# A hand-written order of 1,127 pieces, laid anew: chunked attention with a gated convolution on one core

## The chip, the core and the metric

The kernel runs on one core of a Trainium2 chip. The time is device microseconds (us) of one execution. Before the change the median of 3 runs is 266.01 us (265.45 to 266.56). The engines are PE (TensorE, matmuls), DVE (VectorE), ACT (ScalarE), POOL (GpSimd) and SP, whose queue issues every DMA of this kernel.

## The reference

There are 8 batches, 8 heads, 576 tokens and 64 columns a head. Attention stays inside chunks of 64 tokens; its output, with the heads side by side (512 columns), goes through a gate made by a 5-tap causal convolution over the tokens, a value projection and an output projection, all in f32:

```
scores = scale * (q_c @ k_c.T);  scores -= max(scores)
attn = exp(scores);  attn /= attn.sum() + 1e-09
x = (attn @ v_c)                      # -> (B, S, 512)
gate = sigmoid(sum_k conv_w[k] * x[t - 4 + k])
out = (gate * (x @ w_val)) @ w_out    # two 512 x 512 weights
```

## The kernel before, in words

The 4,608 tokens are taken in nine groups of 512, `g` = 0 to 8. A group's heads come in two halves, `p` = 0, 1, and its 512 columns in four slices of 128 (`c`, `m` or `hp`, 0 to 3). Nothing loops over them: the string `ORDER` lists 1,127 pieces of work, one after the other, and each engine gets its instructions in the order in which they stand there (`keep_in_program_order`). So the table decides what stands behind what on each engine, and a piece that has to wait holds up all that follows it on its engine. The table `SLOTS` (a string of buffer numbers for each name) says which buffer each tile gets. A load goes to one of six buffers `ld` or, for weights, one of four `acc`, and can be issued only when the buffer's last reader is done; SP issues in the order of the table too.

The pieces named below (numbers behind a name are g, then p or a slice):

- `lq`, `lk`, `lv`: loads of q, k, v, 512 KB each. `lw v c`, `lw o c`: load of a 128-row slice of w_val or w_out, 512 KB. The weights arrive as 64-bit words and are put together on the chip.
- `w1` to `w7`, `wb`: the steps of that for one slice. `w1` (POOL or DVE), `w3` and `w5` (ACT) read the loaded buffer; `w7` adds the parts to the f32 weight; `w6` (ACT) and `wb` make its high and low parts `v_hi`, `v_lo`. A `G` behind a name puts the piece on POOL, a `D` on DVE.
- `S` scores (PE, 32 or 64 small matmuls of 64x64), `mx` maximum and `sb` subtraction (DVE), `ex` exponential (ACT), `sm` sum and reciprocal (DVE), `nm` normalization (POOL, or DVE as `nmD`), `T` transpose (PE), `ec` copy of it (ACT), `A` times v (PE, 64 small matmuls). `ea` is the exponential by rows on ACT (16 instructions). Group 0, half 0 runs `S`, `mx`, `T`, `A` and so on in two parts.
- `sp`, `ep`, `xn`, `xe`: for group 0, half 1, the subtraction of maximum and high part is done by PE and ACT.
- `xc`, `xr`, `xd`: from PSUM the copy of x (ACT), its high part (ACT), its low part (DVE).
- `k0` (ACT, POOL or DVE) and `k` (DVE): the five taps of the convolution; `sg` its tanh (ACT).
- `V g m c`: value projection, three matmuls of 512 columns (high x high, low x high, high x low); `F 0 m c` does the same for group 0 with f32 operands as two matmuls.
- `vc`/`gs` or `gm`, `gr`, `gd`: the gated value and its high and low part. `P g t c`: output projection, three matmuls. `oc` copies it out of PSUM, `st` stores it.
- `W n`: n matmuls on a tile of zeros, `zr`, `zi`, `zw`, `zm`: constants.

Work of several groups is in flight at once: group 0 begins with its loads while the weights are still being put together, and from about group 1 on scores of a later group, value matmuls of one and output matmuls of an earlier one stand mixed on PE.

Of the kernel before, what the change touches and what calls it, by code (L numbers as in the profile page):

```python
# [17 lines left out]
ORDER = """lk 0 0,lq 0 0,lc,lw v 0,zr 0,w1G c 0,zw,lk 0 1,S 0 0 1,mx 0 0 1,S 0 0 0,zi,sb 0 0 1,mx 0 0 0,ex 0 0 1,zr 1,lq 0 1,  # L18
w5 v 0,sb 0 0 0,lw v 2,W 5,sm 0 0 1,w1G v 0,nm 0 0 1,w3 c 0,zm,ex 0 0 0,w5 c 0,S 0 1 0,w2 v 0,sm 0 0 0,lv 0 0,S 0 1 1,
w3 v 0,lw v 1,mx 0 1,w3 v 2,lk 1 0,nm 0 0 0,w1G v 2,w5 v 2,w2 c 0,hl 0,lq 1 0,w4 v 0,w4 c 0,T 0 0 0,w7 v 0,ec 0 0 0,  # L20
T 0 0 1,w1 v 1,mh 0 1,w9,A 0 0 0,w2 v 2,xc 0 0 0,lw o 3,w3 v 1,ml 0 1,w2 v 1,sp 0 1,ep 0 1,F 0 2 0,lw v 3,ec 0 0 1,
w4 v 2,lq 1 1,w4 v 1,k0 0 0,w7G v 2,w6 v 2,F 0 3 0,F 0 1 0,sm 0 1,w5 v 1,w7G v 1,A 0 0 1,lv 0 1,S 1 0 0,w1G v 3,
xc 0 0 1,w3G o 3,k 0 0 1,w6 v 0,nmD 0 1,lk 1 1,S 1 0 1,F 0 0 0,T 0 1,mx 1 0,k0 0 1,w5 o 3,F 0 1 1,lw o 0,w5 v 3,
w3 v 3,w1G o 3,F 0 3 1,sb 1 0,ec 0 1,ex 1 0,wb v 2,A 0 1,w2 v 3,k 0 0 4,k 0 0 2,xc 0 1 1,sm 1 0,w1G o 0,xc 0 1 0,
S 1 1 0,w3 o 0,lk 2 0,lq 2 0,xr 0 1,nm 1 0,S 1 1 1,F 0 2 1,k0 0 2,lw o 2,xn 0 1,xe 0 1,mx 1 1,sb 1 1,F 0 0 1,ex 1 1,
w4 v 3,V 0 2 2,V 0 1 2,w7G v 3,k 0 2 3,w5 o 0,sm 1 1,S 2 0 0,S 2 0 1,w3G o 2,w2 o 3,w6 v 3,T 1 0,w6 v 1,ec 1 0,mx 2 0,
V 0 0 2,lk 2 1,V 0 3 2,lq 2 1,lv 1 0,wb v 3,k 0 2 2,lv 1 1,S 2 1 0,sb 2 0,k 0 0 3,S 2 1 1,w2 o 0,ex 2 0,mx 2 1,nm 1 1,
A 1 0,V 0 0 3,k0 0 3,V 0 3 3,xr 1 0,sm 2 0,wb v 0,xc 1 0 1,sb 2 1,vc 0 3,V 0 1 3,V 0 2 3,xc 1 0 0,T 1 1,w1G o 2,
xd 1 0,ex 2 1,V 1 3 0,ec 1 1,sm 2 1,lk 3 0,lq 3 0,vc 0 1,S 3 0 0,S 3 0 1,nm 2 0,k 0 1 2,lw o 1,w2 o 2,wb v 1,A 1 1,
sg 0 0,nm 2 1,xc 1 1 0,V 1 3 1,mx 3 0,lv 2 0,gm 0 0,V 1 1 0,xc 1 1 1,hl 1,lk 3 1,ng 3 0,k 0 2 1,w1G o 1,lk 4 0,  # L30
V 1 1 1,V 1 2 0,xr 1 1,V 1 2 1,xd 1 1,V 1 3 2,w4 o 2,V 1 2 2,V 1 1 2,V 1 3 3,k 0 3 2,V 1 1 3,k 0 2 4,w4 o 0,k 0 1 3,
ea 3 0,k 0 3 4,k 0 1 1,w2 o 1,vc 1 3,T 2 1,lq 3 1,w3G o 1,T 2 0,vc 1 1,rc 3 0,k 0 3 3,w4 o 1,ec 2 0,V 1 0 0,V 1 0 1,
ec 2 1,w5 o 1,S 3 1 0,S 3 1 1,k 0 3 1,A 2 0,V 1 0 2,V 1 2 3,sg 0 2,w5 o 2,k 0 1 4,lq 4 0,mx 3 1,xr 2 0,vc 1 2,w7G o 1,
lv 2 1,sb 3 1,lq 4 1,ex 3 1,V 1 0 3,sg 0 3,k0 1 1,A 2 1,xd 2 0,w4 o 3,V 2 2 0,V 2 3 0,vc 1 0,xc 2 0 0,xc 2 0 1,lq 5 0,
w7 o 0,V 2 3 1,V 2 0 0,gm 0 2,V 2 2 1,V 2 0 1,xr 2 1,lv 3 1,lk 4 1,S 4 0 0,k0 1 2,nm 3 0,sm 3 1,S 4 0 1,gs 0 3,w6 o 1,
xd 2 1,gr 0 2,V 2 2 2,mx 4 0,k0G 1 0,sg 0 1,w7G o 2,k 1 1 3,V 2 0 2,V 2 0 3,w6 o 2,gr 0 0,gs 0 1,gdD 0 0,xc 2 1 0,
xc 2 1 1,sb 4 0,V 2 3 2,w6 o 0,V 2 1 0,w7G o 3,V 2 1 1,w6 o 3,k 1 0 1,S 4 1 0,nm 3 1,S 4 1 1,mx 4 1,k 1 0 4,gr 0 1,
gd 0 2,T 3 1,k 1 1 1,V 2 1 2,k 1 2 2,lv 3 0,vc 2 0,ec 3 1,wb o 0,ng 4 1,wb o 1,k 1 1 4,gdD 0 1,V 2 2 3,lk 5 1,k0 1 3,
k 1 2 3,V 2 1 3,P 0 2 0,vc 2 2,wbD o 2,P 0 1 0,hl 2,k 1 2 1,vc 2 1,k 1 0 3,V 2 3 3,k 1 3 4,k 1 1 2,k 1 3 1,P 0 0 0,
ea 4 1,P 0 0 1,rc 4 1,P 0 2 1,lq 5 1,vc 2 3,P 0 2 2,lk 5 0,P 0 0 2,wbD o 3,k 1 3 3,ex 4 0,T 3 0,k 1 2 4,P 0 1 1,  # L40
ec 3 0,P 0 3 0,A 3 1,k 1 3 2,A 3 0,P 0 3 1,xr 3 1,gr 0 3,k 1 0 2,xr 3 0,xc 3 0 0,sm 4 0,P 0 3 2,xc 3 0 1,P 0 1 2,
gd 0 3,sg 1 3,xcD 3 1 0,P 0 1 3,P 0 0 3,P 0 2 3,xc 3 1 1,sg 1 0,P 0 3 3,xd 3 0,oc 0 1,S 5 0 0,S 5 0 1,oc 0 0,oc 0 2,
xd 3 1,oc 0 3,S 5 1 0,S 5 1 1,V 3 3 0,gs 1 0,V 3 0 0,V 3 2 0,nm 4 1,gr 1 0,k0G 2 2,V 3 0 1,V 3 0 2,V 3 3 1,V 3 2 1,
V 3 0 3,sg 1 2,mx 5 0,V 3 3 2,mx 5 1,V 3 1 0,V 3 1 1,sb 5 0,k0 2 3,nm 4 0,T 4 0,ng 5 1,V 3 2 2,k0 2 1,V 3 2 3,V 3 3 3,
sg 1 1,ea 5 1,T 4 1,vc 3 0,vc 3 3,ec 4 0,gs 1 1,gr 1 1,gd 1 0,P 1 3 0,hl 3,lk 6 0,P 1 2 0,V 3 1 2,k 2 3 2,k 2 2 1,
V 3 1 3,k 2 1 3,lq 6 0,gs 1 2,gr 1 2,k0 3 1,lv 5 0,S 6 0 0,S 6 0 1,ec 4 1,k0G 2 0,k 2 2 2,k 2 0 4,lv 5 1,gs 1 3,
# [28 lines left out]
V 7 2 2,nm 8 0,sg 6 1,oc 4 0,k 7 0 2,st 4 3,k 7 0 1,st 2 2,st 3 1,P 5 0 0,V 7 1 3,ec 8 1,gr 5 3,T 8 0,k0 7 2,gr 5 1,
# [25 lines left out]
    t4="0123456789ab012357468b109a523746081b9a23645708a164a1b9236158b7034a9218",  # L101
# [557 lines left out]
```

## Time and profile before

| | |
|---|---|
| median of 3 runs | 266.01 us |
| profiled execution | 267.69 us |
| its span | 265.9 us |
| PE busy | 251.2 us, 94% |
| DVE busy | 236.3 us, 89% |
| ACT, POOL busy | 188.6 us, 103.3 us |
| loads and stores | 41.97 MB, DMA engines 0.9 to 1.0 busy from 4 to 40 us |
| granted TensorE clock | 1.0 in every stretch but the last 6 us (0.90) |

The profiled execution took 1.79 us more than its span, and 1.68 us more than the median. Times in the trace count from the span's start. A busy PE is not a PE at its peak, since matmuls overlap; from about 75 us on their starts follow each other without a hole.

### The profile page before, as it was taken

The page shows a single profiled execution, that of the slowest core. Times are in us where ns is not written, and L with a number is a line of the kernel's source. Part 1 is how long each engine was busy: PE and PEld are TensorE (multiplying, and loading weights), DVE is VectorE, ACT ScalarE, POOL GpSimd, SP SyncE. Part 2 cuts the span into 40 slices and gives each one's busy share as a digit, 9 for nine tenths or more (in the row PEclk, how much of TensorE's full clock was granted, in tenths as well). Part 3 has the DMA queues.
Part 4 walks back from the last instruction along what each step waited for, and adds up shares of the span by engine and source line. Part 5 has one row for each costly group of instructions (what it writes and reads, how often), then busy time and mean ns, then how long its engine had stood idle before and what let it go on. Part 6 is the DMA issues. An engine that isn't in the chain of part 4 may idle for free. (4 is left out here: it accounts for less than half of the span.)

```text
span 265.9 us, 7860 instructions
## 1 busy us (share of the span) xinstructions
PE 251.2 (94%) x3314; PEld 213.7 (80%) x3315; DVE 236.3 (89%) x329; ACT 188.6 (71%) x440; POOL 103.3 (39%) x90
## 2 busy tenths in 40 slices
...
GB/s 226 402 416 395 360 391 273 81 147 179 212 103 147 155 218 20 262 163 78 83 198 31 247 1 188 172 79 2 2 205 192 2 41 4 197 0 0 81 276 158
DMA packets 14291, 42.47 MB, mean 160 GB/s; under 512 B 1712, under 2 KB 1712, under 8 KB 14256
## 3 DMA queue, kind: packets, MB, share of 16 engines
q1 hardware_dynamic: 14256, 41.97, 43.9%
...
HBM read 32.53 MB, written 9.44 MB: 158 GB/s over the span
## 5 line engine op out<-in xcount | busy, mean ns | idle before, releaser
L158 DVE SCALAR_TENSOR_TENSOR acc<-x,cw,acc 128x516 f32<-128x516 f32 (+1 forms) x144 | 106.2, 780 | 1.2 <-ACT acc L158 0.8
L158 PE MATMUL ps<-t,v_hi 128*128 128x512 f32 x240 | 82.3, 389 | 0.0
L158 PEld LDWEIGHTS ps<-t,v_hi 128*128 128x128 f32 x240 | 45.2, 189 | 7.1 <-issue 0.2
L158 PE MATMUL ps<-t,v_lo 128*128 128x512 f32 x120 | 45.6, 380 | 0.0
L158 PE MATMUL ps<-o_hi,t 128*128 128x512 f32 x124 | 44.3, 382 | 0.1
L158 PEld LDWEIGHTS big<-ld,ld 64*64 64x64 f32 x1152 | 19.4, 139 | 12.5 <-issue 10.7
L158 PE MATMUL big<-ld,ld 64*64 64x64 f32 x1152 | 21.8, 226 | 7.6 <-DMA ld<-in_q 7.1
L158 POOL TENSOR_TENSOR t<-e_row,rs 128x1024 f32<-128x1024 f32 (+1 forms) x13 | 25.1, 1933 | 8.1 <-DVE rs L158 6.5
L158 DVE TENSOR_REDUCE mx<-big 128x16 f32<-128x1024 f32 (+1 forms) x19 | 21.8, 1153 | 7.1 <-PE big L158 6.9
L158 PEld LDWEIGHTS ps<-o_hi,t 128*128 128x128 f32 x124 | 23.4, 189 | 3.8 <-DVE t2o L158 0.5
L158 ACT COPY x<-big 128x512 f32<-128x512 f32 (+3 forms) x44 | 19.4, 497 | 9.2 <-PE big L158 5.0
L158 PEld LDWEIGHTS ps<-t,v_lo 128*128 128x128 f32 x120 | 22.7, 189 | 3.0 <-issue 0.2
L158 ACT ACTIVATE acc<-x,cw 128x516 f32<-128x516 f32 (+1 forms) x27 | 19.9, 745 | 0.1
L158 ACT ACTIVATE t<-acc 128x512 f32<-128x512 f32 (+7 forms) x35 | 15.6, 505 | 5.9 <-DVE acc L158 2.8
L158 PE MATMUL ps<-o_lo,t 128*128 128x512 f32 x52 | 19.7, 379 | 0.0
L158 ACT ACTIVATE e_row<-big,mx 128x64 f32<-128x64 f32 x64 | 19.1, 363 | 0.6 <-DVE mx L158 0.6
L158 ACT ACTIVATE e_row<-e_row 128x1024 f32<-128x1024 f32 (+1 forms) x14 | 14.0, 1012 | 7.0 <-DVE e_row L158 7.0
L158 PEld LDWEIGHTS big<-t,ld 64*64 64x64 f32 x960 | 15.8, 135 | 3.9 <-issue 1.8
L158 PE MATMUL big<-t,ld 64*64 64x64 f32 x960 | 17.5, 220 | 1.0 <-issue 0.7
L158 ACT ACTIVATE t<-big 128x1024 f32<-128x1024 f32 x13 | 13.4, 1035 | 7.0 <-PE big L158 6.9
L158 DVE TENSOR_REDUCE rs<-e_row 128x16 f32<-128x1040 f32 (+1 forms) x15 | 17.4, 1157 | 0.2
L158 ACT CAST t<-big 128x1024 fp32r<-128x1024 f32 x16 | 16.5, 1033 | 1.2 <-PE big L158 1.2
...
## 6 DMA issues: line engine op xcount, KB each, us to landing
...
```

Source lines behind the costliest of these rows:

```text
L158: return tc.keep_in_program_order(fn(*args, **kwargs))
```

## The change

`ORDER` is written anew from its second line to about the last fifth (from `P 5 1 3` on the sequence is the same but for the engine of some pieces), and `SLOTS` with it. The pieces and so the arithmetic stay the same, except for their engine: some 45 of them change it. One more matmul on zeros is added (`W 6` for `W 5`). The loads come in the same order up to the ninth DMA and differ behind it. In the code, `ey` makes its row-sum tile under a condition of its own, and `ea` takes an optional half, which the table doesn't use.

```
 ORDER = """...                 (the table's first lines)
-lk 0 0,lq 0 0,lc,lw v 0,zr 0,w1G c 0,zw,lk 0 1,S 0 0 1,mx 0 0 1,S 0 0 0,zi,sb 0 0 1,mx 0 0 0,ex 0 0 1,zr 1,lq 0 1,
+zr 0,zw,zr 1,lk 0 0,lq 0 0,lc,lw v 0,w1G c 0,lk 0 1,lq 0 1,w1G v 0,lw v 2,zi,w3 c 0,w5 c 0,S 0 0 1,lv 0 0,S 0 0 0,
...
-    ld="012345012340521304251043052314032135041200213523114035",
+    ld="012534012350412152413025315412310251430521453454135025",
-    acc="01230120322301321032013203",
+    acc="01203120322013023102310230",
...
         if (g, p) not in probs:
             probs[g, p] = e_rows[next(e_slot)]
+        if (g, p) not in rss:
             rss[g, p] = tile_of("rs", [P, 16], F32)
...
-    def ea(g, p):
-        for i in range(4):
+    def ea(g, p, b=None):
+        for i in range(4) if b is None else (b, 2 + b):
             ey(g, p, i)
```

What this does to SP's queue behind the ninth DMA: the first fence is before, the second after. `ldN` and `accN` are the buffers, the number behind the underscore a running one; `in_moe_w_val` is `lw v`, `in_moe_w_out` is `lw o`.

```order
L158 DMA acc2_195<-in_moe_w_val 128x1024
L158 DMA ld5_201<-in_k 128x1024
L158 DMA ld0_211<-in_q 128x1024
L158 DMA acc3_252<-in_moe_w_out 128x1024
L158 DMA acc0_266<-in_moe_w_val 128x1024
L158 DMA ld1_270<-in_q 128x1024
L158 DMA ld2_304<-in_v 128x1024
L158 DMA ld3_332<-in_k 128x1024
L158 DMA acc2_367<-in_moe_w_out 128x1024
```

Here the last slice of w_val (`lw v 3`, the second `in_moe_w_val`) is the twelfth 512 KB load (the taps, the third DMA, are small and not counted), and `lw o 0` the sixteenth.

```order
L159 DMA acc2_170<-in_moe_w_val 128x1024
L159 DMA ld4_196<-in_q 128x1024
L159 DMA acc0_204<-in_moe_w_out 128x1024
L159 DMA ld0_217<-in_k 128x1024
L159 DMA ld1_219<-in_v 128x1024
L159 DMA acc3_221<-in_moe_w_val 128x1024
L159 DMA ld2_300<-in_q 128x1024
L159 DMA ld3_308<-in_k 128x1024
L159 DMA ld5_353<-in_q 128x1024
L159 DMA acc2_356<-in_moe_w_out 128x1024
```

The load of v for group 0, half 1 (`in_v`) moved ahead of `lw v 3`, which is now the thirteenth, and q of group 2 ahead of `lw o 0`, now the seventeenth; `lw o 3` moved up to the tenth place, into buffer `acc0`.

POOL's queue over the same stretch, from the second `w1G` of a w_val slice on, before and then after. `w1G` are the `TENSOR_SCALAR` rows of f32 from `acc`, `w7G` the `TENSOR_TENSOR` rows with three `t2` names.

```order
L158 TENSOR_SCALAR t24_204<-acc1_134 128x512
L158 MEMSET x0_209 128x4x4
L158 TENSOR_TENSOR ml0_256<-mx1_197,mh0_230 128x16
L158 TENSOR_TENSOR t23_199<-t23_199,t25_206 128x512
L158 TENSOR_TENSOR t27_254<-t27_254,t28_284 128x512
L158 TENSOR_SCALAR t29_323<-acc0_266 128x512
L158 TENSOR_SCALAR t2a_326<-acc3_252 128x512
```

The sum for slice 1 of w_val (`w7G v 1`, which writes `t27_254`) stands ahead of everything that reads slice 3 (`acc0_266`).

```order
L159 TENSOR_SCALAR t24_215<-acc1_90 128x512
L159 MEMSET x0_231 128x4x4
L159 TENSOR_TENSOR ml0_256<-mx1_213,mh0_254 128x16
L159 TENSOR_SCALAR t27_261<-acc0_204 128x512
L159 TENSOR_TENSOR t25_250<-t25_250,t23_198 128x512
L159 TENSOR_SCALAR t2b_312<-acc3_221 128x512
L159 TENSOR_TENSOR t28_263<-t28_263,t2a_295 128x512
L159 TENSOR_SCALAR t2d_358<-acc0_204 128x512
```

Now `w1G o 3` (`acc0_204`) stands ahead of `w7G v 2` (`t25_250`), and `w1G v 3` (`acc3_221`) ahead of `w7G v 1` (`t28_263`).

PE's queue from the scores of group 1 on, before and then after. `x0` with a `t2` tile is an `F` (its two matmuls are one row), `ldN,ldN` are scores, `t4N,ldN` an `A`.

```order
L158 MATMUL big0_306<-ld5_201,ld0_211 64x64 x32
L158 MATMUL ps2_350<-x0_209,t22_193 128x512
L158 MATMUL big1_352<-ident_61,t42_330 128x128 x8
L158 MATMUL ps1_279<-x0_209,t27_254 128x512
L158 MATMUL ps0_277<-x0_209,t27_254 128x512
L158 MATMUL big0_381<-t43_377,ld2_304 64x64 x32
L158 MATMUL big1_424<-ld3_332,ld1_270 64x64 x32
```

Between the transpose and `A 0 1` stand two `F` with slice 1 (`t27_254`).

```order
L159 MATMUL big0_314<-ld0_217,ld4_196 64x64 x32
L159 MATMUL big1_364<-ident_61,t42_350 128x128 x8
L159 MATMUL ps2_383<-x0_231,t21_140 128x512
L159 MATMUL ps2_383<-x0_231,t28_263 128x512
L159 MATMUL big0_387<-t43_378,ld1_219 64x64 x32
L159 MATMUL big1_426<-ld3_308,ld2_300 64x64 x32
```

Now an `F` with slice 0 (`t21_140`) and one with slice 1 (`t28_263`) stand there.

## Rows read from the trace of the kernel before

**Rows 1.** The page's head: busy time, share of the span, instructions.

```profile
span 265.9 us, 7860 instructions
PE 251.2 (94%) x3314; PEld 213.7 (80%) x3315; DVE 236.3 (89%) x329; ACT 188.6 (71%) x440; POOL 103.3 (39%) x90
```

**Rows 2.** Stretches of 10 us: busy time of each engine, clock, DMA.

```profile
core 0: us, PE busy (x) PEld busy (x) DVE busy (x) ACT busy (x) POOL busy (x), PEclk, DMA share, GB/s
10.00:20.00 10.00, 8.18 (x211) 5.88 (x211) 9.52 (x20) 7.78 (x17) 5.39 (x7) 1.00 1.02 416
20.00:30.00 10.00, 9.91 (x158) 5.99 (x158) 9.89 (x13) 9.09 (x14) 9.16 (x8) 1.00 0.99 376
30.00:40.00 10.00, 9.26 (x223) 7.81 (x223) 9.30 (x12) 8.57 (x15) 9.83 (x7) 1.00 1.01 390
...
100.00:110.00 10.00, 10.00 (x169) 8.80 (x168) 9.86 (x15) 9.79 (x19) 5.13 (x3) 1.00 0.38 120
...
220.00:230.00 10.00, 10.00 (x48) 8.77 (x47) 10.00 (x15) 6.92 (x16) 2.58 (x2) 1.00 0.25 93
```

**Rows 3.** The chain that ended last, its end: start, us, what.

```profile
240.43 0.69 DVE t2o L158
241.12 0.04 issue
241.16 21.00 PE ps L158 x96
```

**Rows 4.** PE in order of time, three holes: start, us, [idle before].

```profile
35.94 0.81 PE L158 MATMUL big<-t,ld 64*64 64x64 f32 x39 [0.73 <-issue]
...
43.33 1.16 PE L158 MATMUL big<-t4b,ld 64*64 64x64 f32 x64 [0.92 <-issue]
...
64.89 0.50 PE L158 MATMUL big<-ld,ld 64*64 64x64 f32 x17 [0.50 <-issue]
```

**Rows 5.** DVE in order of time, its three longest waits behind the opening.

```profile
39.55 1.23 DVE L158 TENSOR_TENSOR t4a<-big,t 128x1024 fp32r<-128x1024 f32 x1 [0.63 <-ACT x L158]
46.63 1.23 DVE L158 TENSOR_TENSOR t<-big,t 128x1024 fp32r<-128x1024 f32 x1 [1.38 <-ACT t L158]
65.43 1.22 DVE L158 TENSOR_REDUCE mx<-big 128x16 f32<-128x1024 f32 x1 [0.83 <-PE big L158]
```

**Rows 6.** The opening in order of time: who waited for a load.

```profile
10.88 1.16 PE L158 MATMUL big<-ld,ld 64*64 64x64 f32 x64 [1.54 <-DMA ld<-in_q]
...
12.04 0.67 ACT L158 ACTIVATE t<-acc 128x512 uint32<-128x512 uint32 x1 [1.29 <-DMA acc<-in_moe_w_val]
```

**Rows 7.** POOL in order of time: `w7G v 2`, `w7G v 1`, `w1G v 3`, `w3G o 3`.

```profile
16.43 1.66 POOL L158 TENSOR_TENSOR t<-t,t 128x512 uint32<-128x512 uint32 x1 [1.99 <-DVE t L158]
19.41 1.98 POOL L158 TENSOR_TENSOR t<-t,t 128x512 uint32<-128x512 uint32 x1 [1.32 <-ACT t L158]
21.36 0.88 POOL L158 TENSOR_SCALAR t<-acc 128x512 f32<-128x512 f32 x1
22.32 2.00 POOL L158 TENSOR_SCALAR t2a<-acc 128x512 uint32<-128x512 f32 x1
```

**Rows 8.** PE in order of time: two `F`, `A 0 1`, and `S 2 0`.

```profile
21.73 1.88 PE L158 MATMUL ps<-x,t 128*128 128x512 f32 x4
23.54 1.30 PE L158 MATMUL big<-t,ld 64*64 64x64 f32 x63
...
29.95 1.16 PE L158 MATMUL big<-ld,ld 64*64 64x64 f32 x64
```

**Rows 9.** DVE in order of time: `w3 o 0`, `mx 1 1`.

```profile
25.69 0.90 DVE L158 TENSOR_SCALAR t2g<-acc 128x512 uint32<-128x512 uint32 x1
26.51 1.21 DVE L158 TENSOR_REDUCE mx<-big 128x16 f32<-128x1024 f32 x1
```

**Rows 10.** DVE, four taps in a row, twice; POOL at the second.

```profile
99.28 2.75 DVE L158 SCALAR_TENSOR_TENSOR acc<-x,cw,acc 128x516 f32<-128x516 f32 x4
...
102.87 3.90 DVE L158 SCALAR_TENSOR_TENSOR acc<-x,cw,acc 128x516 f32<-128x516 f32 x4
...
104.87 1.34 POOL L158 TENSOR_TENSOR t<-t2k,t 128x512 fp32r<-128x512 f32 x1 [11.13 <-ACT t L158]
```

More of the change, by code (lines that the diff above doesn't have):

```diff
@@ L15 @@
 AX = mybir.AxisListType
[L18 to L46, printed above, removed]
@@ L93 @@
[L93 to L101 removed]
+ORDER = """zr 0,zw,zr 1,lk 0 0,lq 0 0,lc,lw v 0,w1G c 0,lk 0 1,lq 0 1,w1G v 0,lw v 2,zi,w3 c 0,w5 c 0,S 0 0 1,lv 0 0,S 0 0 0,
@@ new lines @@
+mx 0 0 1,sb 0 0 1,mx 0 0 0,w3G v 0,w2 c 0,W 6,ex 0 0 1,w4 c 0,sb 0 0 0,S 0 1 0,lw v 1,w5 v 0,ex 0 0 0,sm 0 0 1,w9,
+w2 v 0,S 0 1 1,lq 1 0,w5 v 2,sm 0 0 0,nm 0 0 1,lw o 3,nmD 0 0 0,T 0 0 0,zm,mx 0 1,w1G v 2,lk 1 0,lv 0 1,lw v 3,w4 v 0,
+T 0 0 1,ec 0 0 0,hl 0,A 0 0 0,w3 v 2,w1 v 1,mh 0 1,ml 0 1,w2 v 2,ec 0 0 1,w7 v 0,w1G o 3,w3 v 1,sp 0 1,xc 0 0 0,
+w4 v 2,F 0 2 0,w2 v 1,ep 0 1,w5 o 3,A 0 0 1,xc 0 0 1,w5 v 1,k0 0 0,w7G v 2,lq 1 1,w4 v 1,sm 0 1,F 0 0 0,lk 1 1,
+F 0 3 0,w1G v 3,S 1 0 0,S 1 0 1,k0 0 1,w5 v 3,nmD 0 1,k 0 0 1,lq 2 0,w7G v 1,lw o 0,w3G o 3,lv 1 0,mx 1 0,T 0 1,
@@ new lines @@
+w6 v 2,sb 1 0,k 0 0 2,w3 v 3,ec 0 1,ex 1 0,w6 v 0,wb v 2,F 0 1 0,F 0 1 1,k 0 0 4,A 0 1,w2 v 3,lk 2 1,sm 1 0,S 1 1 0,
+w3 o 0,lk 2 0,S 1 1 1,xr 0 1,xc 0 1 0,xc 0 1 1,nm 1 0,lw o 2,F 0 2 1,k0 0 2,F 0 3 1,mx 1 1,lq 2 1,sb 1 1,xn 0 1,
+xe 0 1,F 0 0 1,V 0 0 2,w4 v 3,w1G o 0,V 0 1 2,ex 1 1,S 2 0 0,k 0 2 3,w7G v 3,w3G o 2,S 2 0 1,T 1 0,w2 o 0,V 0 3 2,
+k0 0 3,w6 v 3,wb v 3,sm 1 1,lk 3 0,nm 1 1,w6 v 1,mx 2 0,V 0 2 2,ec 1 0,k 0 2 2,lq 3 0,sb 2 0,ex 2 0,S 2 1 0,wb v 0,
+w5 o 0,k 0 0 3,S 2 1 1,mx 2 1,lv 1 1,A 1 0,lw o 1,wb v 1,xc 1 0 1,xr 1 0,V 0 1 3,V 0 2 3,vc 0 1,w1G o 2,V 0 0 3,
```

122 lines of the change are left out of this document (71 added, 51 removed).

## The prediction

> **What bounds the kernel now.** I read the page's head first, then the stretches of 10 us, then the chain that ended last, then the idle times of PE and DVE in order of time. The head says PE 94% and DVE 89% busy [rows 1]; since a busy PE is not a PE at its peak, the stretches tell more. From 100 us on PE is busy 10.00 of 10 us, DVE 9.9 to 10.0, at clock 1.00, which is the 2.4 GHz level, while the DMA share is 0.25 to 0.38 [rows 2]. From 10 to 40 us the DMA engines are full (0.99 to 1.02), and PE, DVE and often ACT and POOL have 0.1 to 1.8 us to spare in each ten [rows 2]. So there are two regimes: an opening where the loads and the chains from load to first use decide, and a long body where PE has no room and DVE next to none. The chain's end agrees: from 241.16 us on it is PE alone, 96 matmuls in 21.00 us, released by a DVE copy out of PSUM of 0.69 us [rows 3]. 21.00/96 is 0.219 us a matmul of 512 columns, and no other order makes those shorter.
>
> The price of an edit is therefore the change of PE's idle time before about 75 us, plus any hole that the new order tears into the dense body. What can be won is bounded by what is idle now: PE 1.82, 0.09 and 0.74 us in the three stretches from 10 to 40 us [rows 2], in which the hole of 0.73 us at 35.94 lies, and behind them 0.92 at 43.33 and 0.50 at 64.89 [rows 4]. That makes 4.1 us. DVE's own waits there are 0.63, 1.38 and 0.83 us [rows 5].
>
> **The change part by part.** All sums are against the profiled execution, 267.69 us (span 265.9 and 1.79 around it), which is 1.68 above the median of 266.01.
>
> *The loads.* A full queue lands one 512 KB load every 524,288/416 = 1.26 us [rows 2], and the sixth landed at about 12.04, when ACT got it [rows 6]. So the n-th lands at 12.04 + 1.26 (n - 6), in both orders: the tenth at 17.1, the twelfth 19.6, the thirteenth 20.9, the seventeenth 25.9. The new order cannot make the loads faster, only exchange their places. This presumes that each is issued well ahead. `lw o 3` now needs `acc0`, which is free once POOL's new `w3G v 0` is done: some 8.9 + 2.0 (a `w3G`'s length [rows 7]) = 10.9 us, 6 us before its turn. I take 0 for the issue; the other end is one load's 1.26 us.
>
> *POOL and PE at 20 to 25 us.* `w7G v 1` ran at 19.41 for 1.98 us, before `w1G v 3` at 21.36 [rows 7]. Now `w1G v 3` stands ahead of it and waits for the thirteenth load: 20.9 + 0.7 to 0.9 makes 21.7, and `w7G v 1`, 1.7 to 2.0 long, ends at about 23.5. On PE the first `F` with slice 1 (`F 0 1 1`) now waits for it, and behind it in PE's queue stand `A 0 1`, both halves of `S 1 1` and all that follows. Before, four matmuls (two `F`) ran from 21.73 to 23.6 and `A 0 1` began at 23.54 [rows 8]. Now PE is through with `F 0 1 0` at about 21.9 and idle until 23.5, so `A 0 1` begins at about 24.4: 0.9 us later and with one `F` of 0.9 us less behind it, 1.8 us in work. PE had holes of its own before `S 2 0` at 29.95 [rows 8] that take up about a third of that. On ACT, `w5 o 3` (tenth load, 17.1) and `w5 v 3` (thirteenth, 20.9) wait some 0.3 to 0.5 us each.
>
> *DVE at 25 to 41 us.* `w3 o 0` needs the seventeenth load instead of the sixteenth: 25.9 against its start at 25.69 [rows 9], so 0.2 us; `mx 1 1` at 26.51 [rows 9] and what follows shifts with it. The exponential `ex 1 1` stands on ACT behind `xe 0 1`, which waits for `xn` on PE, late by about 1 us; that may cost DVE's `sm 1 1` another 0.5. Against this stands the wait of 0.63 before `xd 1 0` at 39.55 [rows 5], which such a lateness uses up first, and the 1.38 before `xd 1 1` [rows 5], in which one more tap now runs ahead. I take +0.5 us for the whole front at `A 1 1` (43.33). Below it could be -2.6, all idle PE time up to there gone except the 0.92; above it is 1.8 + 0.5 = +2.3, nothing absorbed.
>
> *Opening.* Half of the first normalization goes from POOL to DVE (0.69, as the copy of that size [rows 3]) and one `w3` from DVE to POOL. The first transpose can start about 0.9 us earlier, but its product waits for v, the seventh load (13.3), and the first `F` for `w7 v 0`, which stands behind `w1 v 1` and so behind the eighth load (14.6). I take 0. The added warm matmul falls into PE's wait of 1.54 us before 10.88 [rows 6]: 0, and 0.4 if that cover were gone.
>
> *Body.* DVE loses 22 instructions and gains 19, most of 0.69 us, with one of 1.22 less and two more: 4 x 0.69 - 1.22 = 1.5 us less work in all. But PE is the bound there, with a backlog of work ready, so I take 0. Below: -0.5 for the hole at 64.89 [rows 4]; above +1.2, since group 4's four score blocks now stand in one piece on PE and DVE's `mx 4 0` behind them would wait that much longer than its 0.83 [rows 5].
>
> *Tail.* Four copies out of PSUM go from DVE to ACT, among them the one that released PE at 241.16 [rows 3]. PE's hole there was 0.3 us; I take -0.3, with 0 and -1.0 as ends (DVE's saving reaching PE whole).
>
> Sum: 0 + 0.5 + 0 + 0 - 0.3 = +0.2, so 267.9 against 267.69, and **266.2 us** in the median.
>
> **Two rules weighed.** The hole of 0.92 us lies where two blocks of 64 small matmuls stand next to each other, with nothing shown as waited for [rows 4]. The Trainium skill (Runtime: NRT & Kernel Launch, Instruction fetch mechanics) says that a sequencer fetches its next 16 KiB of instructions while it runs, mostly hidden. By that rule such a hole must be something else and could go with the order; by the row it stays, because the new order has the same neighbours there (`S 3 0` and `A 1 1`). The sum keeps it; by the rule it would be 0.9 lower.
>
> Four taps on DVE took 2.75 us at 99.28 and 3.90 at 102.87, where a POOL product of two inputs began at 104.87 [rows 10]: one tap was longer by about 1.1 us. The Trainium skill (SBUF — State Buffer, Who interferes with whom) says that a DVE instruction with two SBUF inputs and a POOL one that reads SBUF lock each other out. The trace agrees with it. Here it would let the time scatter by one such lock, 1.1 us, wherever the new order lets the two meet on a chain that gates PE.
>
> **The rivals.**
> - *Faster: the holes close.* If the new order fits the real landings, PE's holes of 0.73 and 0.50 [rows 4], one of DVE's waits of 1.38 [rows 5] in so far as PE follows it, and the 0.3 at the tail go: about -2.5 us, 263.5. For it: the loads decide the first 40 us [rows 2], and v of group 0, half 1, which `A 0 1` needs, is loaded two places earlier. Against: everything behind 75 us is dense already, and the queue hand-walked above shows new waits.
> - *Slower: POOL's new wait.* `w7G v 1` behind the thirteenth load stops PE at `F 0 1 1` for 1.6 us, and the chains behind it (`xn`, `ex 1 1`, `xd 1 0`) pass it on: from there PE has too few holes to take it up, and with ACT's waits it is +2.3: 268.3. It decides as soon as `A 1 1` begins over 1.3 us later than at 43.33.
> - *Nothing moves.* The queue is full until 40 us in both orders, so places are only exchanged, and PE sets the rest: 266.0. This is inside the forecast.
>
> **How the numbers follow.** A change of 0.5%, 1.33 us, is about what can be told from none here. The forecast (within 0.5%) gets 0.39, its own range 264.7 to 267.3. The faster rival gets 0.33: the idle time to be won is real. The slower one gets 0.28. Two in ten lie outside 262.9 to 269.2: below, 266.0 less the 2.6 of the front and 0.5 of the body; above, 266.0 plus 2.3 and half of the body's 1.2 and a little for a lock.
>
> **What would show it.** Right: `w7G v 1` ends near 23.5 us, PE waits for POOL at `F 0 1 1` by 1 to 2 us, `A 1 1` begins within 1 us of 43.33, PE is busy 10.00 in every ten from about 75 us, and the last chain ends in some 96 matmuls again. Wrong: holes of PE behind 75 us (the new body isn't dense), or `A 1 1` more than 1.3 us earlier or later, or the thirteenth load landing well off 20.9.

## The result, and the profile after

The changed kernel takes 269.15 us (median of 4 runs, 268.98 to 269.26) where the kernel before takes 266.28 beside it (4 runs, 265.45 to 267.12): a ratio of 1.0101, 95% interval 1.0068 to 1.0134. It is slower by 2.9 us. The profiled execution took 269.17. That is 0.05 us inside the outer range of the prediction (262.9 to 269.2), and it is there by luck: that upper end was added up from a late front, and the front came early. The forecast, 266.2 within 0.5%, did not come.

The head of the page, and below it stretches of 10 us (columns as in [rows 2]):

```profile
span 267.4 us, 7877 instructions
PE 252.6 (94%) x3316; PEld 212.6 (80%) x3316; DVE 239.7 (90%) x326; ACT 191.6 (72%) x445; POOL 103.0 (39%) x89
```

```profile
10.00:20.00 10.00, 8.22 (x192) 5.38 (x196) 9.82 (x17) 8.05 (x16) 4.85 (x7) 1.00 1.03 417
20.00:30.00 10.00, 8.97 (x182) 5.52 (x174) 9.89 (x13) 8.37 (x13) 7.83 (x6) 1.00 1.02 403
30.00:40.00 10.00, 9.87 (x225) 7.82 (x224) 9.93 (x13) 8.45 (x14) 9.38 (x6) 1.00 0.72 243
70.00:80.00 10.00, 9.17 (x53) 7.33 (x51) 10.00 (x14) 8.16 (x34) 3.67 (x3) 1.00 0.30 110
170.00:180.00 10.00, 9.29 (x58) 7.67 (x60) 9.86 (x15) 8.73 (x41) 2.27 (x2) 1.00 0.31 109
```

DVE has three instructions fewer than before and is busy 3.4 us longer (239.7 against 236.3 [rows 1]). PE has lost 0.83 us in the stretch from 70 to 80 and 0.71 from 170 to 180, and the prediction held it dense from about 75 us on. Between 20 and 30 us it lost 1.03 (0.09 before [rows 2]); 0.72 of that is POOL's new wait, which came where it was forecast, but shorter than the 1.6 forecast. Between 30 and 40 us the DMA engines are no longer full (share 0.72 for 1.01 [rows 2]). PE and POOL in order of time (start, us, [idle before]):

```profile
23.42 1.13 PE L159 MATMUL ps<-x,t 128*128 128x512 f32 x2 [0.72 <-POOL t L159]
24.47 1.16 PE L159 MATMUL big<-t,ld 64*64 64x64 f32 x64
...
41.56 1.16 PE L159 MATMUL big<-ld,ld 64*64 64x64 f32 x64
42.54 1.11 PE L159 MATMUL big<-t4b,ld 64*64 64x64 f32 x64
```

```profile
21.48 0.65 POOL L159 TENSOR_SCALAR t2b<-acc 128x512 f32<-128x512 f32 x1 [1.94 <-DMA acc<-in_moe_w_val]
22.09 1.27 POOL L159 TENSOR_TENSOR t<-t,t2a 128x512 uint32<-128x512 uint32 x1
```

`w7G v 1` ends at 23.36 (23.5 was forecast), PE stands still at `F 0 1 1`, `A 0 1` begins at 24.47 (24.4). The first agreement has two errors in it that cancel: `w1G v 3` waited for its load until 21.48 where 20.9 was forecast for the landing, and the sum itself took 1.27 for 1.7 to 2.0. But `A 1 1` begins at 42.54, earlier than the 43.33 of [rows 4], and the hole of 0.92 ahead of it is gone. The chain that ended last ends in PE alone, with no release from DVE in it as in [rows 3]:

```profile
208.38 55.25 PE ps L159 x255
```

To see where PE fell behind, I summed the work that it had begun by a given time, each matmul at the pace of undisturbed rows (0.2165 us for 512 columns, twice that for an `F`, 0.109 a transpose, 1/64 a 64x64 one), and took the difference to a second trace of the kernel before (first experiment). Positive is ahead, in us; the last column is the last experiment:

```
at us   before, first trace   changed   last experiment
 24          +0.88             -0.80        -0.83
 44          -0.05             +0.57        +0.52
 68          -0.80             +0.46        -0.09
 76          -1.16             -0.59        -0.09
108          -1.16             -1.20        -0.09
156          -1.10             -1.24        -0.09
180          -1.16             -2.86        -0.09
236          -1.16             -2.97        -0.09
260          -1.17             -2.64        +0.25
```

So the new order is half a microsecond ahead at 44 us and still at 68, loses 1.05 by 76, another 0.6 by 108, 1.6 between 156 and 180, and wins 0.33 at the tail. The first trace of before falls 1.16 behind the second, by holes that the second doesn't have (0.92 at 43.33 and 0.50 at 64.89 [rows 4], and 0.33 ahead of 70.89).

Three waits carry most of the loss. First, PE at `T 3 1` and `P 0 1 0` (71.17, 75.66); then DVE ahead of its half of the copy `xc 5 0 1` (138.74); then PE at `T 7 0` (176.17). Each in order of time:

```profile
71.17 1.06 PE L159 MATMUL big<-ident,t4a 128*128 128x128 f32 x8 [0.66 <-DVE e_row L159]
...
75.66 0.48 PE L159 MATMUL ps<-o_hi,t2p 128*128 128x512 f32 x1 [0.17 <-DVE t2p L159]
...
176.17 1.09 PE L159 MATMUL big<-ident,t 128*128 128x128 f32 x8 [0.71 <-ACT e_row L159]
```

```profile
74.25 0.16 DVE L159 TENSOR_SCALAR mx<-mx 128x16 f32<-128x16 f32 x1
...
138.74 0.76 DVE L159 COPY x<-big 128x128 f32<-128x128 f32 x2 [2.02 <-ACT x L159]
...
169.93 1.24 DVE L159 TENSOR_SCALAR mx<-mx 128x16 f32<-128x16 f32 x1
171.09 1.22 DVE L159 TENSOR_REDUCE rs<-e_row 128x16 f32<-128x1040 f32 x1
```

```profile
169.87 1.27 POOL L159 TENSOR_TENSOR t2m<-t2g,t2d 128x512 fp32r<-128x512 f32 x1
```

The row at 169.93 is `ng 7 1`. The same operation took 0.16 us at 74.25. Here it began 0.06 behind POOL's `gd 4 0`, an instruction of two inputs, and ended 0.03 after it: DVE was held for 1.08 us. The 16 exponentials `ea 7 1` on ACT wait for it, they free the PSUM buffer that `T 7 0` takes, and PE stood 0.88 us longer than its matmuls need.

The wait at 71.17 has a like cause, as far as the trace tells. DVE worked without a break up to the two rows that PE waits for there, and two of its taps on the way met POOL and took 1.77 and 1.58 us where a tap takes 0.74 (at 73.59, for one). DVE, then POOL:

```profile
65.48 1.77 DVE L159 SCALAR_TENSOR_TENSOR acc<-x,cw,acc 128x516 f32<-128x516 f32 x1
...
70.94 1.58 DVE L159 SCALAR_TENSOR_TENSOR acc<-x,cw,acc 128x516 f32<-128x516 f32 x1
```

```profile
65.42 1.28 POOL L159 TENSOR_TENSOR o_lo<-t2f,o_hi 128x512 fp32r<-128x512 f32 x1 [1.01 <-ACT o_hi L159]
...
70.69 1.28 POOL L159 TENSOR_TENSOR t2g<-t2e,t 128x512 fp32r<-128x512 f32 x1
```

Together they are 1.9 us too long, and PE lost 1.15 there (0.82 at `T 3 1`, 0.33 at `P 0 1 0`). No run takes these two meetings away.

Another part of the loss has no wait in it. Before, `A 3 1` and `A 3 0` stood side by side on PE, and so did `S 7 1` and `A 6 1`. In the changed order matmuls of 512 columns stand between them, and PE goes into a block of 64x64 matmuls and out of it once more. PE of the changed kernel at `A 3 1` and `A 3 0`, then of the second trace of before:

```profile
79.96 1.16 PE L159 MATMUL big<-t,ld 64*64 64x64 f32 x64
81.05 0.48 PE L159 MATMUL ps<-o_hi,t 128*128 128x512 f32 x1
...
81.89 1.16 PE L159 MATMUL big<-t,ld 64*64 64x64 f32 x64
82.99 0.48 PE L159 MATMUL ps<-o_hi,t2l 128*128 128x512 f32 x1
```

```profile
80.03 1.16 PE L158 MATMUL big<-t,ld 64*64 64x64 f32 x64
81.01 1.11 PE L158 MATMUL big<-t4a,ld 64*64 64x64 f32 x64
82.05 0.48 PE L158 MATMUL ps<-o_hi,t2m 128*128 128x512 f32 x1
```

The two blocks take 1.09 and 1.10 us apart and 2.02 together, and the starts around each are late as well: by the sum of the table the split at 80 us cost 0.36 (-0.58 at 79.6, -0.94 at 83.9), and 0.40 was lost from 158 to 172, around the other one.

### The profile page after: what moved, and what is told of

It reads as the page before. It is cut to its first block, busy times and chain, and to the rows that moved or that the text cites. A ratio compares the mean times of both kernels' runs of the same rounds, so it can differ in the third digit from the quotient of the medians.

```text
span 267.4 us, 7877 instructions
## 1 busy us (share of the span) xinstructions
PE 252.6 (94%) x3316; PEld 212.6 (80%) x3316; DVE 239.7 (90%) x326; ACT 191.6 (72%) x445; POOL 103.0 (39%) x89
## 4 chain that ended last, share of the span: by engine, by line
PE 55%; DVE 30%; DMA 5%; ACT 4%; issue 3%; POOL 1%; SPq 0%; ACTq 0%
PE ps L159 46%; DVE acc L159 11%; PE big L159 9%; DVE mx L159 5%; DVE rs L159 3%; DVE t L159 3%; DVE e_row L159 3%; DMA acc<-in_moe_w_out 3%; DMA acc<-in_moe_w_val 2%; ACT e_row L159 2%; ACT t L159 1%; POOL t L159 1%; DVE t2f L159 1%; DVE t2e L159 1%; DVE t2d L159 1%
## 5 line engine op out<-in xcount | busy, mean ns | idle before, releaser
L159 DVE SCALAR_TENSOR_TENSOR acc<-x,cw,acc 128x516 f32<-128x516 f32 (+1 forms) x144 | 108.9, 794 | 0.4
L159 PE MATMUL ps<-t,v_hi 128*128 128x512 f32 x224 | 78.1, 390 | 0.0
L159 PEld LDWEIGHTS ps<-t,v_hi 128*128 128x128 f32 x224 | 42.1, 189 | 7.0 <-issue 0.2
L159 PE MATMUL ps<-t,v_lo 128*128 128x512 f32 x112 | 42.6, 380 | 0.0
L159 PE MATMUL ps<-o_hi,t 128*128 128x512 f32 x88 | 32.3, 383 | 0.0
L159 ACT COPY t<-ps 128x512 f32<-128x512 f32 x25 | 15.1, 603 | 9.4 <-PE ps L159 9.2
L159 POOL COPY x<-x 128x16 f32<-128x16 f32 x8 | 4.0, 505 | 42.7 <-DVE acc L159 29.5
L159 PEld LDWEIGHTS ps<-o_hi,t 128*128 128x128 f32 x88 | 16.6, 189 | 2.4
L159 PE MATMUL big<-ident,t 128*128 128x128 f32 x128 | 16.8, 274 | 1.2 <-ACT e_row L159 0.7
L159 PEld LDWEIGHTS big<-ident,t 128*128 128x128 f32 x128 | 14.6, 141 | 3.6 <-ACT e_row L159 1.1
```

Source lines behind the costliest of these rows:

```text
L159: return tc.keep_in_program_order(fn(*args, **kwargs))
```

## The experiments

Each time stands against the runs of the kernel before on the same chip (their median in brackets); the changed kernel itself has only its four runs above, so a difference to its 269.15 is less sure than one to the kernel before (whose medians differ by 0.8 between groups). Unless said otherwise, a kernel is the changed one with the edit shown.

**The kernel before, a second trace.**

> The kernel before once more, for a second trace of it. Theory (a): the two holes that PE had in the first trace behind 35 and 42 us (0.73 and 0.92 us beyond the matmuls' own pace, with nothing shown as waited for) are chance; then one or both are missing here, and the span is 1 to 1.7 us below the 265.9 us of the first profile (264.2 to 264.9). Rival (b): they belong to this order; then both stand at the same places with about the same length, and the span is 265.5 to 266.3. Both expect no hole of PE over 0.3 us between 75 and 235 us.

266.52 us, span 264.7. Two of the three holes of [rows 4] are gone: `A 1 1` follows its neighbour at once, and the block at 63.44 runs through. PE in order of time:

```profile
37.00 0.81 PE L158 MATMUL big<-t,ld 64*64 64x64 f32 x39 [0.69 <-issue]
...
42.31 1.16 PE L158 MATMUL big<-ld,ld 64*64 64x64 f32 x64
43.29 1.16 PE L158 MATMUL big<-t4b,ld 64*64 64x64 f32 x64
...
63.44 1.16 PE L158 MATMUL big<-ld,ld 64*64 64x64 f32 x64
```

(a) for 43.33, and so for the one at 64.89, which it did not name; (b) for 35.94, which stands here again with 0.69. The traces hold a cause that these rows call "issue". They list every packet of 16 KiB on the instruction queue, 26 in each trace, and each of the four holes ends 2.37 to 2.47 us after such a packet began (at 33.57, 40.89 and 62.50 in the first trace, at 34.53 here). So does a fifth, of 0.68 at 37.03, in the kernel "old, then new" below. The hole at 43.33 came with a packet at 40.89 and two blocks that start at 41.24; here, with 40.72 and 42.31, there is none. In all likelihood PE waits there for its own instructions; no run tested it. The runs of the kernel before spread by 2 to 4 us on a chip; the four of the changed kernel by 0.3, those of its variants by up to 1.6. So the two first profiles, 1.5 apart, understate the loss: against this trace it is 2.7 (267.4 - 264.7).

**All four `ng` on ACT.**

```
-  run(V.tensor_scalar, out=m, in0=m, scalar1=-SCALE, ...)
+  run(S.mul, m, m, -SCALE)
```

> The changed kernel with one thing replaced: the four small scalings of the row maxima by -1/8 (ng, 128x16) run on ACT instead of DVE. Theory (a): in the changed kernel the one of group 7 (ng 7 1) was held on DVE from 169.93 for 1.24 us, instead of about 0.16, until POOL's product gd 4 0 ended at 171.14; behind it come 16 exponentials on ACT, which free the PSUM buffer that the transposes T 7 0 need, and PE had a hole of 0.88 us at 176.17. With the scaling on ACT the exponentials start about 1 us earlier, the hole at T 7 0 is below 0.2 us, and the time is 0.6 to 1.0 below the changed kernel: 268.2 to 268.6 where that one has 269.15, ratio to the kernel before 1.007 to 1.009. Rival (b): ACT is itself late there (it copies group 4's products before), so the exponentials start as late as before, the hole stays over 0.6 us and the time is 269.0 to 269.4, ratio 1.010 to 1.012. Rival (c): the 0.88 goes but comes back at the next gate of PE, since DVE is the one that is behind: no hole at T 7 0, another of the same length before 205 us, time 269.0 to 269.4.

269.24 (265.52), ratio 1.0127, 1.0088 to 1.0166: (b). On ACT the scaling waits for `mx 7 1` and holds up two copies and a cast behind it, so the exponentials begin at 171.32, as in the changed kernel (171.27):

```profile
169.68 0.22 ACT L159 ACTIVATE mx<-mx 128x16 f32<-128x16 f32 x1 [2.57 <-DVE mx L159]
...
171.32 0.34 ACT L159 ACTIVATE e_row<-big,mx 128x64 f32<-128x64 f32 x1
```

The edit swapped one wait for another; it tells nothing on the hold's price. That had to be asked again (below).

**Two halves put together, cut at `A 6 0` (145 us).** New, then old:

> The changed kernel's list up to the product A 6 0 of group 6 (about 145 us), and from there the pieces that are left in the order of the kernel before (buffers from there on dealt out anew, the one longest free first). Theory (a): the loss sits in the new order between 150 and 185 us, since PE's progress was level in the two traces from 100 to 152 us and 1.8 us behind at 184; then this kernel is like the kernel before or a little better, 265.6 to 267.0, ratio 0.998 to 1.003. Rival (b): the new front has left DVE and ACT behind with work that PE needs only later; then the holes come at 155 to 185 us all the same, with 268 to 269.5, ratio 1.007 to 1.012. What speaks against reading it too closely is the joint: if a hole of PE stands right behind 145 us, it belongs to that.

Old, then new:

> The reverse: the list of the kernel before up to A 6 0 of group 6 (about 145 us), and from there the pieces that are left in the changed kernel's order, with its engines in the tail (buffers from there on dealt out anew). Theory (a), the loss sits in the new order between 150 and 185 us: a hole of PE at T 7 0 again (0.5 to 1.2 us) and one or two of 0.3 to 0.7 before it, time 267.2 to 269.2, ratio 1.004 to 1.011. Rival (b), the new front has left the engines behind: no such holes, and with the 0.3 us that the new tail saves 265.3 to 266.3, ratio 0.997 to 1.001.

New, then old: 276.84 (265.52), ratio 1.0406, 1.0357 to 1.0455. Both theories missed. PE had one hole of 6.15 us, 8 us behind the cut, and it waited for ACT, which waited for DVE (ACT and PE, then DVE, in order of time):

```profile
158.04 1.06 ACT L157 ACTIVATE e_row<-e_row 128x1024 f32<-128x1024 f32 x1 [7.02 <-DVE e_row L157]
...
159.62 0.80 PE L157 MATMUL ps<-o_hi,t2b 128*128 128x512 f32 x1 [5.99 <-ACT t L157]
```

```profile
147.38 5.47 DVE L157 SCALAR_TENSOR_TENSOR acc<-x,cw,acc 128x516 f32<-128x516 f32 x5
...
156.78 1.23 DVE L157 TENSOR_TENSOR e_row<-big,mx 128x1024 f32<-128x1024 f32 x1
```

The last row is `sb 7 0`. The second trace of before has it at 145.3: here DVE had taps of the earlier groups still to do. After the hole the granted clock is 0.50 from 159 to 161 us, the 1.2 GHz level, and the next matmuls start 0.43 apart, which is 1.5 us more. Much of the 6 us belongs to the joint, as the expectation warned; it points at DVE as the engine that the new front leaves behind.

Old, then new: 266.92 (265.52), ratio 1.0032, 1.0004 to 1.0059. No hole at `T 7 0`, so (a) is wrong: that hole does not belong to the new last part alone. With the old front DVE arrives with room to spare, in stretches of 10 us from 150 on 8.92, 8.08 and 9.35 busy where the changed kernel has 9.97, 9.96 and 9.86. The time is 0.6 above what (b) gave. PE waits for nothing here, and yet by the sum of the table it loses 0.71 between 140 and 172: two blocks stand apart that were side by side, `S 7 0` and `A 6 0` at the joint, `A 6 1` and `S 7 1` by the new order.

**DVE's wait at 138.74, and its hold at 169.93, apart and together.**

```
- xc 5 0 0,xcD 5 0 1,xd 5 1        (xcD: on DVE)
+ xc 5 0 0,xc 5 0 1,xd 5 1         (on ACT)
```

> The changed kernel with one instruction pair moved: the copy xc 5 0 1 (two of 128x128) is done by ACT, as in the kernel before, instead of DVE. In the changed kernel DVE waited 2.02 us for ACT in front of it (at 138.74), and xd 5 1 stood behind. Theory (a), the time is lost because DVE falls behind what PE needs from 135 us on: DVE's wait there shrinks to under 0.7 us, mx 7 1 (168.68 in the changed kernel) begins 1 to 2 us earlier, the hole of PE at T 7 0 (0.88 at 175 to 176) is under 0.3, and the time is 0.8 to 1.7 below the changed kernel's: 267.4 to 268.4, ratio to the kernel before 1.002 to 1.009 by the two measurements of that so far (266.28 and 265.52). Rival (b), the hole hangs on where POOL's products meet DVE and not on DVE's place: the hole stays over 0.5 and the time is 268.8 to 269.5. Rival (c), ACT is late instead (0.6 us more on it): another wait of the same size on xd 5 1 or k0 5 1, time 268.8 to 269.8.

```
- mx 7 1,P 3 0 1,ng 7 1, ... oc 3 3,xc 6 1 1,ea 7 1
+ mx 7 1,P 3 0 1, ... oc 3 3,xc 6 1 1,ngS 7 1,ea 7 1      (ngS: the same on ACT)
```

> The changed kernel with the scaling ng 7 1 (128x16) alone moved from DVE to ACT, and there put right in front of the 16 exponentials ea 7 1, so that nothing of ACT's queue waits behind it that did not before (with all four moved and left in their places, the cast behind it waited 2.57 us for mx 7 1 and the exponentials began at 171.32 as before). Theory (a), the hold of 1.24 us on DVE is worth what PE loses at T 7 0: the exponentials begin at 170.0 to 170.4 instead of 171.27, the hole at T 7 0 falls from 0.88 to under 0.2, time 268.2 to 268.6. Rival (b), DVE is behind as a whole: the exponentials begin earlier, but what DVE next owes PE is late, so a hole comes back before 200 us, time 268.8 to 269.5.

> Both edits together: xc 5 0 1 on ACT, and ng 7 1 on ACT right in front of ea 7 1. Theory (a), DVE's lag from 135 us on is the cause: no hole of PE over 0.3 us between 80 and 235 us, time 266.8 to 267.9, that is 1.3 to 2.3 below the changed kernel and within 0.8 us of the kernel before or better. Rival (b), other waits take their place: 268.4 to 269.4.

Against 266.20: the copy on ACT 268.25 (ratio 1.0074, 1.0049 to 1.0099), `ng 7 1` on ACT 268.10 (1.0055, 1.0030 to 1.0081), both 268.23 (1.0069, 1.0045 to 1.0092). Each alone takes off about 1 us, and the two together no more: by the sum of the table PE loses 1.77 from 108 to 236 us in the changed kernel and 0.82 to 0.83 in each of the three. The rows say why. With the copy on ACT, DVE's wait is 0.31 instead of 2.02, and `ng 7 1` comes 0.56 earlier and is no longer held; with `ng 7 1` on ACT the exponentials begin at 169.74. Either way `T 7 0` follows without a hole. DVE of the first kernel, then ACT and PE of the second:

```profile
136.95 1.23 DVE L159 TENSOR_TENSOR t4a<-big,t 128x1024 fp32r<-128x1024 f32 x1 [0.31 <-ACT t L159]
...
169.37 0.17 DVE L159 TENSOR_SCALAR mx<-mx 128x16 f32<-128x16 f32 x1
```

```profile
169.74 0.31 ACT L159 ACTIVATE e_row<-big,mx 128x64 f32<-128x64 f32 x1
...
174.63 0.38 PE L159 MATMUL ps<-t,v_hi 128*128 128x512 f32 x1
174.84 1.04 PE L159 MATMUL big<-ident,t 128*128 128x128 f32 x8
```

So the hole at `T 7 0` is worth its 0.9 us, as (a) of the first two had it (the times are inside its range for the copy, 0.1 below it for `ng 7 1`), and it has two causes of which either must go. The third, 268.23, lies between its two ranges. What its (a) expected fails: with the copy on ACT, DVE's gain of 1.4 us (`mx 7 0` at 145.9 instead of 147.3) is down to 0.6 at `mx 7 1` (168.11, not the 1 to 2 expected), where DVE then waits 0.40 for PE; and PE has a new hole of 0.36 at 140.93, which ACT releases. Between 80 and 235 us these traces show no second hole of DVE's making to be won.

**POOL's order at 20 us put back.**

```
- F 0 3 0,w1G v 3, ... lq 2 0,w7G v 1,lw o 0,w3G o 3
+ F 0 3 0,w7G v 1,w1G v 3, ... lq 2 0,lw o 0,w3G o 3
```

> The changed kernel with w7G v 1 back in front of w1G v 3 on POOL, the order of the kernel before at this place; all else as in the changed kernel. PE's wait of 0.72 to 1.1 us at F 0 1 1 (23.4 us) goes. Theory (a), what was lost there was made up before 45 us, since the holes behind it took it in: A 1 1 begins within 0.5 us of 42.54, time within 0.4 us of the changed kernel, 268.7 to 269.5. Rival (b), the slower rival of the prediction: POOL's wait passes through to the end, and without it the time is 267.3 to 268.0.

270.84 (266.20), ratio 1.0158, 1.0123 to 1.0192: slower than the changed kernel by 1.5 (ratios) to 1.7 (times), which neither theory had. POOL's sum `w7G v 1` now runs where DVE normalizes half of group 0 and does a tap. POOL, then DVE:

```profile
19.39 2.27 POOL L159 TENSOR_TENSOR t<-t,t2a 128x512 uint32<-128x512 uint32 x1
21.63 1.13 POOL L159 TENSOR_SCALAR t2b<-acc 128x512 f32<-128x512 f32 x1
```

```profile
18.34 2.19 DVE L159 TENSOR_TENSOR t<-e_row,rs 128x1024 f32<-128x1024 f32 x1
20.45 1.76 DVE L159 SCALAR_TENSOR_TENSOR acc<-x,cw,acc 128x512 f32<-128x512 f32 x1
```

In the changed kernel the same sum takes 1.27 and `w1G v 3` 0.65 (rows above), and the tap 0.74; the normalization took 2.03 there too, beside an earlier instruction of POOL. PE gets `A 0 1` no earlier (24.70 against 24.47): ahead of it stands a hole of 1.25 that nothing in the trace releases, 2.17 us after a packet of instructions began. DVE is 1.7 behind the changed kernel by 30 us, PE has a hole of 1.04 at 35 us instead of none, and `A 1 1` begins at 44.16. So in this order POOL's new wait was the cheaper of the two places; what the wait costs by itself this run does not show.

**`T 3 1` two products later, without and with `ng 7 1` on ACT.**

```
- P 0 2 0,...,vc 2 1,T 3 1,w6 o 3,V 2 0 2,V 2 2 3,ec 3 1
+ P 0 2 0,...,vc 2 1,w6 o 3,V 2 0 2,V 2 2 3,T 3 1,ec 3 1
```

> The changed kernel with one piece later on PE: the transposes T 3 1 stand behind V 2 0 2 and V 2 2 3 instead of ahead of them. In the changed kernel both halves of group 4's scores stand in the two PSUM buffers of 1024 columns, and T 3 1 waited at 71.17 (0.82 us beyond the matmuls' pace) until DVE's subtraction sb 4 0 was through with one. Two products of 0.65 us each now fill that wait. Theory (a), every hole that PE has there is lost to the end, since PE is dense behind it: the hole goes and the time is 0.6 to 0.9 below the changed kernel: 268.2 to 268.6. Rival (b), it is DVE that is behind and sets when PE ends: PE runs ahead there and loses it again at the next gates (P 0 2 1 at 75.66, P 3 3 0 at 156, T 7 0 at 176), holes there longer by 0.5 or more in sum, time 268.8 to 269.4.

> The changed kernel with two edits: T 3 1 behind two products as in the run before, and ng 7 1 on ACT right in front of ea 7 1. Theory (a), the two holes of 0.82 and 0.88 us are separate losses: 1.5 to 1.9 below the changed kernel, 267.2 to 267.7. Rival (b), DVE's lag is what counts: no better than with ng 7 1 alone, 267.9 to 268.5.

269.24 (266.20), ratio 1.0116, 1.0085 to 1.0146; and 268.32, 1.0091, 1.0060 to 1.0122: (b) both times. The wait moves to the next pieces instead of going. PE in order of time, first `T 3 1`, then `T 3 0`, then `P 0 1 0`:

```profile
71.82 1.04 PE L159 MATMUL big<-ident,t4a 128*128 128x128 f32 x8
...
73.97 1.09 PE L159 MATMUL big<-ident,t 128*128 128x128 f32 x8 [0.47 <-ACT t L159]
...
75.85 0.48 PE L159 MATMUL ps<-o_hi,t2p 128*128 128x512 f32 x1 [0.35 <-DVE t2p L159]
```

One of the two large PSUM buffers is held by `S 4 1` until its exponentials are done, so `T 3 1` and `T 3 0` go through the other one after the other; and `P 0 1 0` waits for DVE in any case.

**The new opening with the old body.** The changed kernel's list up to `A 1 1` (42.5 us), then the old order:

> The changed kernel's list up to A 1 1 (about 42.5 us; its loads, its order on POOL, its wait at F 0 1 1), and from there the pieces that are left in the order of the kernel before (buffers from there on dealt out anew). Theory (a), the new opening is 0.5 us better at 44 us (PE's progress against the second trace of the kernel before: +0.57) and what is lost is lost behind it: no hole of PE over 0.6 us behind 45 us, and 265.3 to 266.3, ratio to the kernel before 0.995 to 1.001. Rival (b), the new opening leaves DVE or ACT behind and the loss follows from it whatever comes after: 267 to 269, ratio 1.004 to 1.012, with holes at the joint or at 70 us.

269.56 (266.20), ratio 1.0124, 1.0083 to 1.0165: above both ranges. The profiled execution was one of the two fastest (268.18; the runs go up to 271.20). The joint has a hole of 2.19, as (b) allowed. Behind it there is none over 0.25 us up to the end: PE's progress against the second trace is -1.63 at 68 and -1.62 at 236. PE, then DVE:

```profile
49.67 0.70 PE L157 MATMUL ps<-t,v_hi 128*128 128x512 f32 x2 [2.03 <-DVE t L157]
```

```profile
44.23 1.79 DVE L157 SCALAR_TENSOR_TENSOR acc<-x,cw,acc 128x512 f32<-128x512 f32 x1
...
48.41 1.21 DVE L157 TENSOR_TENSOR t<-big,t 128x1024 fp32r<-128x1024 f32 x1
```

**The joint mended, and the new tail.** Two taps behind `xd 1 1` on DVE, and fourteen pieces from `P 5 1 3` on with the changed kernel's engines (the bar is the joint):

```
- gm 0 0 | k 0 1 2,A 1 1, ... ng 3 0,k 0 2 1, ... xd 1 1
+ gm 0 0 | A 1 1, ... ng 3 0, ... xd 1 1,k 0 1 2,k 0 2 1
- ocD 5 3, ocD 5 2, ocD 6 1, ocD 8 2, gd 6 3, ...
+ oc 5 3,  oc 5 2,  oc 6 1,  oc 8 2,  gdD 6 3, ...
```

> The changed kernel's list up to A 1 1, then the order of the kernel before as in the run before, with two more edits: on DVE the taps k 0 1 2 and k 0 2 1 stand behind xd 1 1 instead of ahead of it (in the run before PE had a hole of 2.19 us at 47.3, waiting for xd 1 1, which DVE began at 48.41 behind those taps), and the tail from P 5 1 3 on has the changed kernel's engines (its four copies out of PSUM on ACT, and ten more of its choices). Theory (a), the new opening is 0.5 us better, the old body holds PE dense, and the new tail closes the hole at 241 us: the hole at 47 us falls under 0.3, no other over 0.4 behind it, PE's last matmul starts at 260.0 to 260.9, time 265.5 to 266.3, ratio to the kernel before 0.996 to 1.001. Rival (b), the opening leaves DVE some 1.2 us of work behind, and PE, no longer held at 47 us, meets that at 60 to 75 or 150 to 185 us: holes of 0.8 to 2 us there in sum, time 266.8 to 268, ratio 1.002 to 1.008.

266.49 (266.01), ratio 1.0018, 0.9998 to 1.0037. Nearest to (a): the joint's hole is 0.15, PE dense from 60 us on (last column of the table), the tail's 0.33 won; but the time is 0.2 above what (a) gave. It beats the changed kernel by 2.7 us, and not the kernel before: a hole of 0.63 at 57.5, which (a) did not allow, takes the opening's half microsecond back.

## Why the prediction was right and wrong

**The front: right to within 0.2 us at 24, wrong in its sum.** `w7G v 1` ended and `A 0 1` began as worked out (23.36 for 23.5, 24.47 for 24.4), the first by two errors that cancel. PE's wait was 0.72, not 1.6, since `F 0 1 0` began at 21.68 and was not through at 21.9. PE was 1.7 us behind the first trace of before (from +0.88 to -0.80 in the table), which is the 1.8 of the prediction, but only 0.8 behind the second. I took +0.5 for what would be left at `A 1 1`; it was -0.8 (42.54 against 43.33, and 43.29 in the second trace). The holes behind took it up whole.

**The two rules.** The hole of 0.92 at 43.33, which the sum kept because the new order has the same neighbours there, is absent with those neighbours in the changed kernel (41.56, 42.54) and even in the kernel before when traced again. The Trainium skill (Runtime: NRT & Kernel Launch, Instruction fetch mechanics) has the fetch mostly hidden. Most of the 26 packets in each trace agree with it; the holes of 0.50 to 0.92, each 2.4 us behind the start of one, look like those that are not hidden. That also fits a hole which comes and goes with the same neighbours. The prediction took "mostly hidden" to mean that the hole must be something else. The second rule I called a source of scatter. It is not: an order fixes who meets whom. Take as the usual length of a DVE row the median of its operation and shape in the two traces of before and the one of the changed kernel. Every row that is over 0.15 us longer runs beside a POOL row, in all three. By 80 us that excess sums to 6.1 us in the changed kernel against 2.7 in the second trace of before, by 190 to 10.6 (18 rows) against 3.7 (8 rows); and the hold of `ng 7 1`, 1.24 us in the changed kernel, stands again with 1.23 in two of its variants. The Trainium skill (SBUF — State Buffer, Who interferes with whom) also says that a scaling by a scalar, one input, can take the shared pair of ports in its fast mode and is then blocked for the whole of the other's instruction. The row of `ng 7 1` agrees: 1.24 for 0.16, until POOL's end. I had weighed the rule only for instructions with two inputs.

**The body: the step that failed.** "But PE is the bound there, with a backlog of work ready, so I take 0." PE lost 3.4 us between 68 and 236 (+0.46 to -2.97). My upper end of +1.2, for group 4's four score blocks in one piece, named the right place: 1.05 went there. What I did not price is that DVE at 9.9 of 10 us [rows 2] has no room either, though I had written that it has next to none. I counted 1.5 us less work on it, by usual lengths (1.0 by the medians); it was busy 3.4 longer, since its excess beside POOL over the whole execution is 13.9 us against 9.3 in the first trace of before. How much of DVE's work is done by a given time is no measure of that lateness: at 190 us the changed kernel is 5.1 us of usual work behind the second trace of before, and "old, then new" is 4.3 behind without a hole at `T 7 0`, because the new order places DVE's pieces later. Where the old body stands behind the same opening, PE holds; where the new last part stands behind the old front, it nearly holds (1.0032); so most of the loss arises in the new order between 44 and 145 us and is paid in part behind it. Shown by runs is the 0.9 at `T 7 0`, by two kernels. The 1.05 at 68 to 76 has its place and, by the rows alone, its cause: two taps of DVE that met POOL. Of the 1.4 from 76 to 108 and from 156 to 172 the traces give some 0.7 to the two pairs of blocks taken apart and 0.3 to one wait for ACT at 156.37; the rest is small, and no run here takes any of it away one by one.

**The tail: right.** -0.3 forecast, 0.33 measured, in the changed kernel and in the last experiment. The working left out that two copies (`oc 7 3`, `oc 7 0`) go the other way, from ACT to DVE.

**The rivals.** The slower one came true in its number (268.3 against 269.15), not in its mechanism: POOL's wait was there and did not pass on, and undoing it made the kernel slower still. The point from which it decides, `A 1 1` later than 43.33 by 1.3, was not reached. The sign I had named for a wrong forecast, holes of PE behind 75 us, is what the trace shows. Of the faster rival's 2.5 us about 0.9 came: the hole at 36 us, which the kernel before has in both traces, is gone (+0.07 at 36, +0.67 at 40 by the same sum), and the 0.33 at the tail. Its 0.50 at 64.89 stood in one trace of before and not in the other. "Nothing moves" held the queue full until 40 us in both orders; it was not, from 30 us on (0.72).
